# Four more attention units transposed on VectorE and scaled by rows on ScalarE, in a Strassen-type matmul kernel

## The chip, the cores and the metric

The kernel runs on one core of one Trainium2 chip. The metric is the device time of one execution in microseconds (us), as the median of the runs. PE is TensorE, DVE VectorE, ACT ScalarE, POOL GpSimd, SP SyncE, whose queue issues the transfers.

## The reference

The input is attention in blocks of 64 tokens, for 8 batches, 8 heads, 576 tokens and a head of 64, and behind it a two-layer network with a gate:

```
scores = q_c @ k_c.T / 8            # per block of 64 tokens
attn   = softmax(scores)            # rows of 64, minus their maximum
out    = attn @ v_c
x      = out as (4608 tokens, 512)
h      = x @ w_in                   # 512 -> 2048
g      = h * clip(h + 3, 0, 6) / 6
y      = g @ w_out                  # 2048 -> 512
```

All of it is float32. Products are taken in three passes of a split into a high part and a rest (`passes`, lines 376 to 380), so that one tile of 128 x 128 by 512 costs three matmuls.

## The kernel before

The 4608 tokens are nine column blocks of 512 (n = 0 to 8). Attention of one block is two **units**, named by block and half: "30" is block 3, first half. A unit has 16 score matrices of 64 x 64 per pair of lanes, held as 128 lanes x 1024 columns in two PSUM banks.

Blocks 1 and 2, 3 and 4, 5 and 6, 7 and 8 form pairs, and the two matmul layers of a pair (or of the part of it that is not done plainly) use seven products in place of eight, with sums and differences of quarters of the weights and of x (Strassen's method in Winograd's form). Each product of the first layer is called f, of the second s: `f6.0.5` is product 6 of the first layer for the first pair, rows 5. The four sums of quarters of a weight tile are made by `combine` (lines 480 to 482) on DVE: four operations on 256 columns each, the next on the result of the last, for 16 weight tiles (`whole`, `comb`, `top`, `less`, `send`, lines 880 to 884). They are split into a high part and a rest, stored to DRAM and loaded again by later pairs.

The steps of a unit (lines 661 to 694):

- `scores` on PE; a unit's scores follow the product of the unit before it in one piece (`products`).
- `max`: the largest of each row, on DVE.
- Either `less`, `exp`, `sum` (one DVE subtraction, one ACT exponential of 1024 columns, one DVE sum of the rows with a small addition and a reciprocal), or, for the units in `ROWS`, `negate`, `exp0_` to `exp7_`, `invert`: 16 ACT exponentials of 64 columns, each with its own bias and with its sum accumulated.
- `share`: DVE multiplies the 1024 columns with the reciprocals.
- Either `turn` and `turned` (eight transposes of 128 x 128 on PE into PSUM and one ACT copy), or, for the units in `FLIPPED`, `flip`, `save`, `down`, `up`: one DVE transposition in blocks of 32 x 32 from PSUM into SBUF, and five ACT copies of 512 columns that put the blocks in their places (lines 312 to 324). A flipped unit keeps its exponentials in PSUM, in the place of the scores, and its scores are laid out in another order (lines 246 to 252).
- `product` on PE into two banks, then `keep`, an ACT copy of them.

Before the change units 30, 31, 40 and 41 are in `ROWS` and not in `FLIPPED`; unit 21 is in neither.

**The order** is not written by hand: `Schedule.order` (lines 105 to 149) takes all steps with a cost, the steps they depend on and a due time, subtracts from each due time the costs of the steps behind it, and lists them greedily per engine. All engines then issue in this order. The PSUM banks are rings: `h` has two, `o` four. A product of a unit that stands among the f and s products (`PLACES`, line 726) takes both banks of `h`, in a place of the ring that is fixed (unit 30 behind the first group of f products, 31, 40 and 41 behind the first, third and fifth s product). The next product that uses `h` (numbers 6 and 3) waits until these banks are read, that is until the unit's `keep`.

Of the kernel before, what the change touches and what calls it, by code (L numbers as in the profile page):

```python
# [43 lines left out]
LAG = 2  # L44
ROWS = ["30", "31", "40", "41", "60", "61", "80", "81"]
XDVE = ["x0.s0c", "x0.s2", "x0.s2b", "x0.s3", "x0.s3b"]
# [19 lines left out]
LATE = (5, 9)  # L66
FLIPPED = ("50", "51", "60", "61", "70", "71", "80", "81")

# [71 lines left out]
def tile_kernel(ctx: ExitStack, tc: tile.TileContext, qk_in, v_in, weights, out):  # L140
# [84 lines left out]
    class Attention:  # L225
# [67 lines left out]
        def share(self):  # L293
            DVE.tensor_tensor(out=self.flat(self.e), in0=self.flat(self.e), in1=self.wide(self.z), op=ALU.mult)

        def soft(self, step):
            for f in ((self.largest,), (self.lessen, self.exp), (self.total,), (self.share,))[step]:
                f()
# [161 lines left out]
    parked = {}  # L460

    def sum_steps(m, p):
        cols = lambda k: slice(256 * k, 256 * k + 256)
        t = {}

        def q(row, col):
            f, k = quarter(m, row, col)
            return t["a"][:, f, cols(k)]

        def whole():  # L470
            t["a"] = sp.tile([P, 2, 512], F32, name="a")
            for f in range(2):
                if in_dram(m, p):
                    nc.sync.dma_start(out=t["a"][:, f], in_=astore["ab"[m] + str((p + NFP * f) // 2)][:, p % 2])
                else:
                    h, l = [w_of(m, p + NFP * f)[:, k].bitcast(F32) for k in range(2)]
                    DVE.tensor_tensor(out=t["a"][:, f], in0=h, in1=l, op=ALU.add)

        def combine(engine):
            for to, x, y, op in ((q(1, 1), q(1, 0), q(1, 1), ALU.add), (q(1, 0), q(0, 0), q(1, 0), ALU.subtract),  # L480
                                 (q(0, 0), q(1, 1), q(0, 0), ALU.subtract), (q(0, 1), q(0, 1), q(0, 0), ALU.subtract)):
                engine.tensor_tensor(out=to, in0=x, in1=y, op=op)

        def high():
            t["hl"] = parked[m, p] = hp.tile([P, 2, 2, 2, 256], F32R, name="hl")
            t["s"] = t["a"].rearrange("p f (k t) -> p f k t", k=2)
            ACT.copy(out=t["hl"][:, :, :, 0], in_=t["s"])

        def lower(engine):
            engine.tensor_tensor(out=t["hl"][:, :, :, 1], in0=t["s"], in1=t["hl"][:, :, :, 0].bitcast(F32), op=ALU.subtract)  # L490

        def send():
            for i, row, col in ((5, 1, 1), (7, 1, 0), (6, 0, 0), (3, 0, 1)):
                f, k = quarter(m, row, col)
                nc.sync.dma_start(out=kept(m, p, i), in_=t["hl"][:, f, k].rearrange("p l t -> p (l t)").bitcast(F32))

        def send_own():
            for i, row, col in ((1, 0, 0), (2, 0, 1), (4, 1, 1)):
                f, k = quarter(m, row, col)
                to = kept(m, p, i).rearrange("p (l t) -> p l t", l=2)  # L500
                nc.sync.dma_start(out=to, in_=w_of(m, p + NFP * f)[:, :, cols(k)].bitcast(F32))

        return whole, combine, high, lower, send, send_own
# [48 lines left out]
    def x_steps(s):  # L552
        n = NSTD + 2 * s
        b = lambda i, j: xraw[n + j][:, i]
        name = lambda i: f"x{s}.{i}"
        minus = lambda to, x, y, on=DVE: lambda: on.tensor_tensor(out=b(*to), in0=b(*x), in1=b(*y), op=ALU.subtract)
        sub = ("DVE", 1.22)
        ops[s] = {}
        last = name("s0")
        sub_on = lambda k: ("POOL", 2.5) if k in XPOOL else sub  # L560
        steps = [(last, *sub_on("s0"), [], minus((0, 1), (0, 1), (0, 0), POOL if "s0" in XPOOL else DVE), [0, 1])]

# [7 lines left out]
        for i in ORDER_A:  # L570
            reads = {2: [3], 3: [2]}.get(i, [])
            steps.append((name(f"{i}h"), "ACT", 1.05, [last], lambda slot, i=i: high(i, slot), reads))
            steps.append((name(f"{i}l"), "DVE", 1.22, [name(f"{i}h")], lambda i=i: lower(i), []))
            for k, at, to, x, y, reads in (("s1", 5, (0, 1), (1, 1), (0, 1), [2]), ("s2", 6, (0, 0), (0, 1), (0, 0), []),
                                           ("s3", 6, (0, 1), (1, 0), (0, 1), [3])):
                if i == at:
                    steps.append((name(k), *sub_on(k), [name(f"{i}l"), name("1l"), last], minus(to, x, y, POOL if k in XPOOL else DVE), reads))
                    last = name(k)
# [4 lines left out]
    def first_x_steps():  # L583
# [9 lines left out]

        def from_banks(u, i, y):
            def f():
                for (to, part), (less, _) in zip(heads[u].parts(t(i)), heads[u].parts(y())):
                    DVE.tensor_tensor(out=to, in0=part, in1=less, op=ALU.subtract)
            return f
# [12 lines left out]
        of = lambda i: lambda: t(i)  # L611
        work.add("x0.s0", "DVE", 1.22, ["product20", "rest10", "c7", "own6", "own7"], from_banks("20", 5, x(1, 0, 0)), due=due_of["20"])
        work.add("x0.s1", "DVE", 1.38, ["product21", "x0.s0c"], from_banks("21", 6, of(5)), due=due_of["21"])
        for name, i, one, two, kind, after in (("x0.s0c", 5, of(5), x(1, 0, 1), ALU.subtract, ["x0.s0"]),
                                               ("x0.s2", 7, of(6), x(1, 0, 0), ALU.subtract, ["x0.s1", *left(15)]), ("x0.s2b", 7, of(7), x(1, 0, 1), ALU.subtract, ["x0.s2"]),
                                               ("x0.s3", 4, x(1, 1, 0), of(6), ALU.subtract, ["x0.s1", "rest11", *left(15)]), ("x0.s3b", 4, of(4), x(1, 1, 1), ALU.add, ["x0.s3"])):
            on = name not in XDVE
            work.add(name, "POOL" if on else "DVE", 2.7 if on else 1.22, after, op(POOL if on else DVE, i, one, two, kind))
# [14 lines left out]
    def weight_of(p, i):  # L633

        if i in (1, 2, 4):
            return w_of(0, p + NFP * (i == 4))[:, :, 256 * (i != 1):256 * (i != 1) + 256]
        row, col = {5: (1, 1), 7: (1, 0), 6: (0, 0), 3: (0, 1)}[i]
        return parked[0, p][:, row, col]
# [13 lines left out]
    def attention(u, due, scores=(), less=(), keep=(), bank=None):  # L652
# [10 lines left out]
        if u in ROWS:  # L663
            rows = [("negate", "DVE", 0.12, a.negate, ()), *[(f"exp{k}_", "ACT", 0.62, lambda k=k: a.exps(k, e() if k == 0 else None), less if k == 0 and u not in FLIPPED else ()) for k in range(8)],
                    ("invert", "DVE", 0.45, a.invert, ())]
        steps = [("scores", "PE", 1.30, a.scores, ["qk" + u, *scores]), ("max", "DVE", 1.23, a.largest, ()), *rows, ("share", "DVE", 1.22, a.share, ()), *([("flip", "DVE", 1.22, a.flip, less), ("save", "ACT", 0.56, lambda: a.swap(0), ()), ("down", "ACT", 1.0, lambda: a.swap(1), ()), ("up", "ACT", 1.0, lambda: a.swap(2), ())]
                   if u in FLIPPED else [("turn", "PE", 1.07, a.turn, ()), ("turned", "ACT", 1.02, a.turned, ())]), ("product", "PE", 2.26 if after else 1.50, products if after else a.product,
# [196 lines left out]
    for u in [*range(NFP), *range(NFP + NPL, 2 * NFP), *range(NFP, NFP + NPL)]:  # L864
# [5 lines left out]
        work.add(f"whole{u}", *(("SP", 1.57) if in_dram(m, p) else ("DVE", 1.28)), ["room", *work.take("a", 2, f"whole{u}", [f"less{u}s"])], whole)  # L870
        work.add(f"comb{u}", *(("POOL", 4.2, [f"whole{u}"], lambda f=combine: f(POOL)) if u in COMBS else ("DVE", 1.88, [f"whole{u}"], lambda f=combine: f(DVE))))
        work.add(f"top{u}", "ACT", 1.05, [f"comb{u}", *work.take("hl", 2, f"top{u}", [f"send{u}", *last])], high)
        work.add(f"less{u}s", *(("POOL", 2.5, [f"top{u}"], lambda f=lower: f(POOL)) if u in LESS_ON_POOL else ("DVE", 1.22, [f"top{u}"], lambda f=lower: f(DVE))), due=due)
# [34 lines left out]
    def first_product(s):  # L908
# [5 lines left out]
        for p in range(0 if s else NPL, NFP):  # L914
# [5 lines left out]
            for k, i in enumerate(ORDER_A):  # L920
# [48 lines left out]
                elif i in (3, 4):  # L969
# [3 lines left out]
                    if i == 3 and s:  # L973
                        work.add(id_("t1."), "POOL", 1.45, [id_("gate3."), id_("gate2.")], lambda f=gq: POOL.tensor_tensor(  # L974
                            out=f(0, 1), in0=f(0, 1), in1=f(0, 0), op=ALU.subtract))
                        work.add(id_("t2."), "POOL", 1.45, [id_("t1."), id_("gate7.")], lambda f=gq, p=p: POOL.tensor_tensor(  # L976
                            out=t2_of(p), in0=f(1, 1), in1=f(0, 1), op=ALU.subtract))
            place_at(("f", s, p), bank_h)

    def add_units(s):  # L980
# [5 lines left out]
        if s == 0:  # L986
            for p in range(NFP):
# [4 lines left out]
                work.add(f"t2.0.{p}", *(("POOL", 1.45) if TPOOL else ("DVE", 0.69)), [f"t1.0.{p}", f"gate{2 * NFT + NFP + p}" if p < NPL else f"gate7.0.{p}", *free], lambda p=p: (POOL if TPOOL else DVE).tensor_tensor(  # L992
                    out=t2_of(p), in0=gate_of(1, 1, p), in1=gate_of(0, 1, p), op=ALU.subtract))
        made_by = {1: "gate2.", 5: "t1.", 6: "t2.", 2: "gate4.", 3: "gate7."}
        for i in ORDER_B:
            for pp in range(NFP // 2):
# [16 lines left out]
                if i == 5:  # L1013
                    work.add(f"m{s}.7.{pp}", "DVE", 1.22, [f"ul{s}.1.{pp}", *both("t2.", pp)], lambda pp=pp: DVE.tensor_tensor(
                        out=gates_of(0, 0, pp), in0=t2s_of(pp), in1=gates_of(0, 0, pp), op=ALU.subtract))
                elif i == 6:
# [137 lines left out]
```

## Time and profile before

| | |
|---|---|
| runs before | 775.85, 776.64, 776.96 us; median 776.64 |
| profiled execution | 776.96 us, span 775.1 us |
| busy | PE 766.4, DVE 644.4, ACT 432.3, POOL 70.6 us |
| chain that ended last | PE 93%, DVE 3%, DMA 2%, ACT 1% |
| PE transposes (L306) of all units | 80 of 128 x 128 |
| sums of quarters (L482) | 64 on DVE, 27.0 us |

A view by stretches gives, for each stretch of the span, the busy time of each engine. A timeline row gives the start, the duration and the instruction; in brackets stands the idle time of that engine before it and what ended it. PE's matmuls are pipelined, so that the time between two starts, not the duration, is what one costs. On DVE and ACT an instruction may start up to some 0.1 us before the end of the one ahead of it.

### The profile page before, as it was taken

What the parts mean: (1) busy time and instruction counts of PE and PEld (TensorE: products, weight loads), DVE (VectorE), ACT (ScalarE), POOL (GpSimd) and SP (SyncE); (2) the same over time, 40 slices, a digit from 0 to 9 for tenths busy, and PEclk for the clock granted to TensorE, in tenths of its full rate; (3) what the DMA queues carried; (4) which work ended last, traced back from release to release, by engine and by line L of the source; (5) the groups of instructions that cost most, each with busy time, mean ns of one, the idle gap of its engine ahead of it and who ended that gap; (6) DMA issues with size and microseconds to landing.
All of it is one profiled execution on the core that took longest, in us unless ns stands there. A gap on an engine that the chain in (4) does not pass through costs nothing.

```text
span 775.1 us, 14046 instructions
## 1 busy us (share of the span) xinstructions
PE 766.4 (99%) x5538; PEld 628.8 (81%) x5540; DVE 644.4 (83%) x812; ACT 432.3 (56%) x749; POOL 70.6 (9%) x55
## 2 busy tenths in 40 slices
PE   8999999999999999999999999999999999999998
PEld 4788888887888888888888888888888888888887
DVE  6999999999999999967999788678997657679751
ACT  3998843565667654537785535466945333355330
POOL 0000000000000000231300003221200013222000
PEclk9999999999999999999999999999999999999999
DMA  9999999877859997567677785667667666566672
GB/s 369 395 395 342 349 342 319 283 237 232 283 203 334 336 367 266 195 194 255 204 257 248 251 288 191 227 220 261 202 199 232 208 215 198 196 197 204 197 234 92
DMA packets 69426, 198.06 MB, mean 256 GB/s; under 512 B 7024, under 2 KB 19568, under 8 KB 65008
## 3 DMA queue, kind: packets, MB, share of 16 engines
q1 hardware_dynamic: 69216, 197.03, 74.2%
q8 instruction: 44, 0.72, 0.4%
q14 instruction: 22, 0.18, 0.1%
q10 hardware_dynamic: 144, 0.13, 0.1%
HBM read 153.09 MB, written 44.04 MB: 254 GB/s over the span
## 4 chain that ended last, share of the span: by engine, by line
PE 93%; DVE 3%; DMA 2%; ACT 1%; issue 1%; SPq 0%; DVEq 0%; ACTq 0%
PE acc L378 21%; PE acc L379 21%; PE acc L380 21%; PE h L378 8%; PE h L380 8%; PE h L379 8%; PE h L346 2%; PE two L256 1%; PE two L251 1%; PE two L306 1%; DMA b<-hl 1%; DMA out_t<-u 1%; PE h L174 1%; PE two L346 1%; PE h L394 0%
## 5 line engine op out<-in xcount | busy, mean ns | idle before, releaser
L378 PE MATMUL acc<-wa,ws 128*128 128x512 f32 (+1 forms) x536 | 208.8, 390 | 0.1
L380 PE MATMUL acc<-wa,ws 128*128 128x512 f32 (+1 forms) x536 | 207.8, 388 | 0.0
L379 PE MATMUL acc<-wa,ws 128*128 128x512 f32 (+1 forms) x536 | 207.8, 388 | 0.0
L1007 ACT CAST wa<-wb 128x1024 fp32r<-128x1024 f32 x96 | 99.8, 1051 | 74.6 <-PE acc L380 46.1
L1011 DVE TENSOR_TENSOR wa<-wb,wa 128x1024 fp32r<-128x1024 f32 x96 | 120.3, 1271 | 17.7 <-ACT wa L1007 17.5
L378 PEld LDWEIGHTS acc<-wa,ws 128*128 128x128 f32 x536 | 100.7, 188 | 21.7 <-DVE u L900 0.5
L380 PEld LDWEIGHTS acc<-wa,ws 128*128 128x128 f32 x536 | 100.7, 188 | 20.6
L379 PEld LDWEIGHTS acc<-wa,ws 128*128 128x128 f32 x536 | 100.7, 188 | 20.3
L974 POOL TENSOR_TENSOR wb<-wb 128x512 f32<-128x512 f32 x24 | 33.8, 1407 | 628.7 <-DVE wb L788 621.8
L785 ACT ACTIVATE r<-acc,half 128x512 f32<-128x512 f32 x90 | 61.5, 686 | 31.2 <-DVE acc L900 26.8
L785 ACT ACTIVATE r<-h,half 128x512 f32<-128x512 f32 x38 | 26.1, 687 | 91.2 <-DVE h L900 83.9
L788 DVE SCALAR_TENSOR_TENSOR wb<-r,acc 128x512 f32<-128x512 f32 x90 | 61.1, 683 | 6.7 <-ACT r L785 6.2
L379 PE MATMUL h<-wa,ws 128*128 128x512 f32 (+1 forms) x144 | 55.2, 383 | 0.0
L380 PE MATMUL h<-wa,ws 128*128 128x512 f32 (+1 forms) x144 | 55.2, 383 | 0.0
L378 PE MATMUL h<-wa,ws 128*128 128x512 f32 (+1 forms) x144 | 55.2, 383 | 0.0
L900 DVE TENSOR_TENSOR u<-h,p 128x512 f32<-128x512 f32 x32 | 21.9, 686 | 27.7 <-PE h L380 22.7
L900 DVE TENSOR_TENSOR acc<-acc,u 128x512 f32<-128x512 f32 x48 | 33.2, 696 | 6.2 <-PE acc L380 6.2
L976 POOL TENSOR_TENSOR g<-wb,wb 128x512 f32<-128x512 f32 x24 | 36.1, 1504 | 1.9
L788 DVE SCALAR_TENSOR_TENSOR wb<-r,h 128x512 f32<-128x512 f32 x38 | 25.9, 681 | 11.8 <-ACT r L785 11.8
L378 PE MATMUL acc<-wa,wa 128*128 128x512 f32 x88 | 34.9, 397 | 0.2 <-DVE h L900 0.2
L379 PE MATMUL acc<-wa,wa 128*128 128x512 f32 x88 | 34.3, 390 | 0.0
L380 PE MATMUL acc<-wa,wa 128*128 128x512 f32 x88 | 34.3, 390 | 0.0
(211 smaller groups left out, 1420.7 us busy)
## 6 DMA issues: line engine op xcount, KB each, us to landing
ws<-b SPq DMA_DIRECT2D x84, 512.0 KB, 4.7
ws<-a SPq DMA_DIRECT2D x72, 512.0 KB, 4.4
qk<-qk_in SPq DMA_DIRECT2D x17, 1024.0 KB, 7.5
wa<-b SPq DMA_DIRECT2D x28, 512.0 KB, 6.1
a<-wa SPq DMA_DIRECT2D x40, 256.0 KB, 6.2
v<-v_in SPq DMA_DIRECT2D x17, 512.0 KB, 5.3
wa<-w_in_out SPq DMA_DIRECT2D x8, 1024.0 KB, 12.2
wb<-w_in_out SPq DMA_DIRECT2D x8, 1024.0 KB, 9.8
```

The source lines that it names most:

```text
L174: PE.matmul(idle, lhsT=nought.broadcast_to([P, P]), rhs=nought.broadcast_to([P, NT]), start=True, stop=True)
L346: PE.matmul(po[s][o, a, i, :], lhsT=self.v[rows, a, i, o], rhs=self.aT[rows, a, i, o], start=True, stop=True)
L378: PE.matmul(ps, lhsT=a_h, rhs=b_h, start=first, stop=False, skip_group_check=more)
L379: PE.matmul(ps, lhsT=a_h, rhs=b_l, start=False, stop=False, skip_group_check=more)
L380: PE.matmul(ps, lhsT=a_l, rhs=b_h, start=False, stop=last, skip_group_check=more)
L785: ACT.activation(out=t["r"], in_=ps(), func=AF.Relu, bias=half, scale=1.0 / 6.0)
L788: work.add("gate" + name, "DVE", 0.69, ["relu" + name, *more], lambda: DVE.scalar_tensor_tensor(out=out(), in0=t["r"], scalar=1.0, in1=ps( ...
L900: return lambda: DVE.tensor_tensor(out=out(), in0=x(), in1=y(), op=ALU.add)
L974: work.add(id_("t1."), "POOL", 1.45, [id_("gate3."), id_("gate2.")], lambda f=gq: POOL.tensor_tensor(out=f(0, 1), in0=f(0, 1), in1=f(0, 0) ...
L976: work.add(id_("t2."), "POOL", 1.45, [id_("t1."), id_("gate7.")], lambda f=gq, p=p: POOL.tensor_tensor(out=t2_of(p), in0=f(1, 1), in1=f(0, ...
L1007: ACT.copy(out=g_ops[s, i, pp][:, :, 0], in_=src())
L1011: work.add(low, *(("POOL", 2.5) if on else ("DVE", 1.22)), [high], lambda i=i, pp=pp, src=src, on=POOL if on else DVE: on.tensor_tensor(ou ...
```

## The change

Unit 21 joins `ROWS`. Units 30, 31, 40 and 41 join `FLIPPED`. The same four are in a new list `SCALED`: their `share` on DVE is replaced by four steps `scale0_` to `scale3_` on ACT, each of four products of 64 columns with a column of the reciprocals. In `combine` two of the four sums, with other signs, become one operation on 512 columns with one operand repeated; the other two stay at 256 columns, and the three are steps of their own. With the signs, the four sums stand at other quarters (`SUM_AT`), and seven kinds of subtraction or addition elsewhere, on operands of the same shape, change their sign.

```diff
-ROWS = ["30", "31", "40", "41", "60", "61", "80", "81"]
+ROWS = ["21", "30", "31", "40", "41", "60", "61", "80", "81"]
+SCALED = ["30", "31", "40", "41"]
-FLIPPED = ("50", "51", "60", "61", "70", "71", "80", "81")
+FLIPPED = ("30", "31", "40", "41", "50", "51", "60", "61", "70", "71", "80", "81")
...
+        def scale(self, k):
+            for c in range(4 * k, 4 * k + 4):
+                ACT.mul(self.flat(self.e)[:, c], self.flat(self.e)[:, c], self.z[:, c:c + 1])
...
+    SUM_AT = {5: (1, 0), 7: (0, 0), 6: (1, 1), 3: (0, 1)}
...
-        def combine(engine):
-            for to, x, y, op in ((q(1, 1), q(1, 0), q(1, 1), ALU.add), (q(1, 0), q(0, 0), q(1, 0), ALU.subtract),
-                                 (q(0, 0), q(1, 1), q(0, 0), ALU.subtract), (q(0, 1), q(0, 1), q(0, 0), ALU.subtract)):
-                engine.tensor_tensor(out=to, in0=x, in1=y, op=op)
+        def combine(k):
+            if k:
+                to, x = ((1, 1), (0, 0)) if k == 1 else ((0, 1), (1, 1))
+                DVE.tensor_tensor(out=q(*to), in0=q(*to), in1=q(*x), op=ALU.subtract)
+                return
+            four = t["a"].rearrange("p f (k t) -> p (f k) t", k=2)
+            DVE.tensor_tensor(out=four[:, 0:2] if m else four[:, 0:3:2], in0=q(1, 0).unsqueeze(1).broadcast_to([P, 2, 256]), in1=four[:, 0:4:3], op=ALU.subtract)
...
-            for i, row, col in ((5, 1, 1), (7, 1, 0), (6, 0, 0), (3, 0, 1)):
+            for i, (row, col) in SUM_AT.items():
...
-        steps = [..., ("share", "DVE", 1.22, a.share, ()), *([("flip", ...), ("save", ...), ("down", ...), ("up", ...)]
+        steps = [..., *([(f"scale{k}_", "ACT", 0.82, lambda k=k: a.scale(k), ()) for k in range(4)] if u in SCALED else [("share", "DVE", 1.22, a.share, ())]), *([("flip", ...), ...]
...
-        work.add(f"comb{u}", *(... ("DVE", 1.88, [f"whole{u}"], lambda f=combine: f(DVE))))
-        work.add(f"top{u}", "ACT", 1.05, [f"comb{u}", ...], high)
+        work.add(f"comb{u}", "DVE", 0.67, [f"whole{u}"], lambda f=combine: f(0))
+        work.add(f"comb{u}b", "DVE", 0.525, [f"comb{u}"], lambda f=combine: f(1))
+        work.add(f"comb{u}c", "DVE", 0.525, [f"comb{u}b"], lambda f=combine: f(2))
+        work.add(f"top{u}", "ACT", 1.05, [f"comb{u}c", ...], high)
```

## Rows read from the trace of the kernel before

**Rows 1.** The page: busy us of each engine, share, instructions

```profile
PE 766.4 (99%) x5538; PEld 628.8 (81%) x5540; DVE 644.4 (83%) x812; ACT 432.3 (56%) x749; POOL 70.6 (9%) x55
```

**Rows 2.** By stretches: length, busy of PE, PEld, DVE, ACT, POOL, clock, DMA, GB/s

```profile
0.00:30.00 30.00, 25.67 (x400) 16.26 (x403) 20.72 (x24) 17.52 (x22) 0.74 (x7) 1.00 0.95 380
30.00:175.00 145.00, 145.00 (x1126) 119.45 (x1125) 139.69 (x192) 100.22 (x147) 0.00 (x0) 1.00 0.93 328
175.00:180.00 5.00, 4.33 (x30) 2.83 (x32) 4.90 (x10) 2.48 (x3) 0.00 (x0) 1.00 0.61 203
200.00:280.00 80.00, 80.00 (x721) 66.56 (x720) 78.33 (x106) 55.41 (x144) 0.00 (x0) 1.00 0.86 293
```

**Rows 3.** Timeline of PE around the turn of unit 30: start, us, instruction

```profile
174.59 1.03 PE L306 MATMUL two<-ident,e 128*128 128x128 f32 x8
...
175.80 0.50 PE L378 MATMUL acc<-xd,hl 128*128 128x512 f32 x1 [0.18 <-DVE g L900]
```

**Rows 4.** Timeline of PE around the turn of unit 31

```profile
224.37 1.04 PE L306 MATMUL two<-ident,e 128*128 128x128 f32 x8
225.16 0.47 PE L378 MATMUL acc<-wa,wa 128*128 128x512 f32 x1
225.47 0.40 PE L379 MATMUL acc<-wa,wa 128*128 128x512 f32 x1
225.71 0.40 PE L380 MATMUL acc<-wa,wa 128*128 128x512 f32 x1
```

**Rows 5.** Timeline of DVE, unit 21 and one combination of quarters (L482)

```profile
122.91 1.22 DVE L267 TENSOR_TENSOR e<-two,m 128x1024 f32<-128x1024 f32 x1
124.05 1.79 DVE L482 TENSOR_TENSOR a<-a 128x256 f32<-128x256 f32 x4
125.77 1.21 DVE L274 TENSOR_REDUCE z<-e 128x16 f32<-128x1024 f32 x1
127.01 0.18 DVE L275 TENSOR_SCALAR z<-z 128x16 f32<-128x16 f32 x1
...
127.51 1.23 DVE L294 TENSOR_TENSOR e<-e,z 128x1024 f32<-128x1024 f32 x1
```

**Rows 6.** By line: ns min/median/max, first and last start, forms

```profile
L482 DVE TENSOR_TENSOR a<-a x64: 416/425/428, 107.1 to 265.8; 128x256 f32<-128x256 f32 x64
...
L314 DVE STREAM_TRANSPOSE e<-two x8: 1240/1242/1245, 318.4 to 581.4; 128x1024 f32<-128x1024 f32 x8
...
L324 ACT COPY e<-e x16: 615/618/625, 320.3 to 584.6; 32x512 f32<-32x512 f32 x16
```

**Rows 7.** Timeline of ACT, exponentials by rows of unit 30

```profile
154.97 0.31 ACT L286 ACTIVATE e<-two,m 128x64 f32<-128x64 f32 x1
155.16 0.20 ACT L286 ACTIVATION_READ_ACCUMULATOR e<-two,m 128x1 f32 x1
155.26 0.31 ACT L286 ACTIVATE e<-two,m 128x64 f32<-128x64 f32 x1
```

**Rows 8.** Timelines of ACT and PE: keeps of units 30, 31, 41, next h products, unit 40

```profile
180.96 1.07 ACT L359 COPY xa<-h 128x512 f32<-128x512 f32 x2
184.72 0.39 PE L378 MATMUL h<-wa,hl 128*128 128x512 f32 x1
...
230.65 1.07 ACT L359 COPY xa<-h 128x512 f32<-128x512 f32 x2 [1.61 <-PE h L346]
235.70 0.39 PE L378 MATMUL h<-wa,wa 128*128 128x512 f32 x1
...
250.51 1.01 ACT L310 COPY e<-two 128x1024 f32<-128x1024 f32 x1
253.00 1.16 PE L346 MATMUL h<-e,v 64*64 64x64 f32 x64
...
278.21 1.07 ACT L359 COPY xb<-h 128x512 f32<-128x512 f32 x2
285.51 0.39 PE L378 MATMUL h<-wa,wa 128*128 128x512 f32 x1
```

More of the change, by code (lines that the diff above doesn't have):

```diff
@@ L555, in x_steps @@
         name = lambda i: f"x{s}.{i}"
-        minus = lambda to, x, y, on=DVE: lambda: on.tensor_tensor(out=b(*to), in0=b(*x), in1=b(*y), op=ALU.subtract)
+        mix = lambda to, x, y, kind, on=DVE: lambda: on.tensor_tensor(out=b(*to), in0=b(*x), in1=b(*y), op=kind)
         sub = ("DVE", 1.22)
@@ L560, in x_steps @@
         sub_on = lambda k: ("POOL", 2.5) if k in XPOOL else sub
-        steps = [(last, *sub_on("s0"), [], minus((0, 1), (0, 1), (0, 0), POOL if "s0" in XPOOL else DVE), [0, 1])]
+        steps = [(last, *sub_on("s0"), [], mix((0, 1), (0, 1), (0, 0), ALU.subtract, POOL if "s0" in XPOOL else DVE), [0, 1])]
         def high(i, slot):
@@ L573, in x_steps @@
             steps.append((name(f"{i}l"), "DVE", 1.22, [name(f"{i}h")], lambda i=i: lower(i), []))
-            for k, at, to, x, y, reads in (("s1", 5, (0, 1), (1, 1), (0, 1), [2]), ("s2", 6, (0, 0), (0, 1), (0, 0), []),
-                                           ("s3", 6, (0, 1), (1, 0), (0, 1), [3])):
+            for k, at, to, x, y, kind, reads in (("s1", 5, (0, 1), (1, 1), (0, 1), ALU.add, [2]), ("s2", 6, (0, 0), (0, 1), (0, 0), ALU.add, []),
+                                                 ("s3", 6, (0, 1), (1, 0), (0, 1), ALU.subtract, [3])):
                 if i == at:
-                    steps.append((name(k), *sub_on(k), [name(f"{i}l"), name("1l"), last], minus(to, x, y, POOL if k in XPOOL else DVE), reads))
+                    steps.append((name(k), *sub_on(k), [name(f"{i}l"), name("1l"), last], mix(to, x, y, kind, POOL if k in XPOOL else DVE), reads))
                     last = name(k)
@@ L592, in first_x_steps, with from_banks @@
         ops[0] = {}
-        def from_banks(u, i, y):
+        def from_banks(u, i, y, kind):
             def f():
                 for (to, part), (less, _) in zip(heads[u].parts(t(i)), heads[u].parts(y())):
-                    DVE.tensor_tensor(out=to, in0=part, in1=less, op=ALU.subtract)
+                    DVE.tensor_tensor(out=to, in0=part, in1=less, op=kind)
             return f
@@ L611, in first_x_steps @@
         of = lambda i: lambda: t(i)
-        work.add("x0.s0", "DVE", 1.22, ["product20", "rest10", "c7", "own6", "own7"], from_banks("20", 5, x(1, 0, 0)), due=due_of["20"])
-        work.add("x0.s1", "DVE", 1.38, ["product21", "x0.s0c"], from_banks("21", 6, of(5)), due=due_of["21"])
+        work.add("x0.s0", "DVE", 1.22, ["product20", "rest10", "c7", "own6", "own7"], from_banks("20", 5, x(1, 0, 0), ALU.subtract), due=due_of["20"])
+        work.add("x0.s1", "DVE", 1.38, ["product21", "x0.s0c"], from_banks("21", 6, of(5), ALU.add), due=due_of["21"])
         for name, i, one, two, kind, after in (("x0.s0c", 5, of(5), x(1, 0, 1), ALU.subtract, ["x0.s0"]),
-                                               ("x0.s2", 7, of(6), x(1, 0, 0), ALU.subtract, ["x0.s1", *left(15)]), ("x0.s2b", 7, of(7), x(1, 0, 1), ALU.subtract, ["x0.s2"]),
+                                               ("x0.s2", 7, of(6), x(1, 0, 0), ALU.add, ["x0.s1", *left(15)]), ("x0.s2b", 7, of(7), x(1, 0, 1), ALU.add, ["x0.s2"]),
                                                ("x0.s3", 4, x(1, 1, 0), of(6), ALU.subtract, ["x0.s1", "rest11", *left(15)]), ("x0.s3b", 4, of(4), x(1, 1, 1), ALU.add, ["x0.s3"])):
@@ L636, in weight_of @@
             return w_of(0, p + NFP * (i == 4))[:, :, 256 * (i != 1):256 * (i != 1) + 256]
-        row, col = {5: (1, 1), 7: (1, 0), 6: (0, 0), 3: (0, 1)}[i]
+        row, col = SUM_AT[i]
         return parked[0, p][:, row, col]
@@ L665, in attention @@
                     ("invert", "DVE", 0.45, a.invert, ())]
-        steps = [("scores", "PE", 1.30, a.scores, ["qk" + u, *scores]), ("max", "DVE", 1.23, a.largest, ()), *rows, ("share", "DVE", 1.22, a.share, ()), *([("flip", "DVE", 1.22, a.flip, less), ("save", "ACT", 0.56, lambda: a.swap(0), ()), ("down", "ACT", 1.0, lambda: a.swap(1), ()), ("up", "ACT", 1.0, lambda: a.swap(2), ())]
+        steps = [("scores", "PE", 1.30, a.scores, ["qk" + u, *scores]), ("max", "DVE", 1.23, a.largest, ()), *rows, *([(f"scale{k}_", "ACT", 0.82, lambda k=k: a.scale(k), ()) for k in range(4)] if u in SCALED else [("share", "DVE", 1.22, a.share, ())]), *([("flip", "DVE", 1.22, a.flip, less), ("save", "ACT", 0.56, lambda: a.swap(0), ()), ("down", "ACT", 1.0, lambda: a.swap(1), ()), ("up", "ACT", 1.0, lambda: a.swap(2), ())]
                    if u in FLIPPED else [("turn", "PE", 1.07, a.turn, ()), ("turned", "ACT", 1.02, a.turned, ())]), ("product", "PE", 2.26 if after else 1.50, products if after else a.product,
@@ L870, in tile_kernel @@
         work.add(f"whole{u}", *(("SP", 1.57) if in_dram(m, p) else ("DVE", 1.28)), ["room", *work.take("a", 2, f"whole{u}", [f"less{u}s"])], whole)
-        work.add(f"comb{u}", *(("POOL", 4.2, [f"whole{u}"], lambda f=combine: f(POOL)) if u in COMBS else ("DVE", 1.88, [f"whole{u}"], lambda f=combine: f(DVE))))
-        work.add(f"top{u}", "ACT", 1.05, [f"comb{u}", *work.take("hl", 2, f"top{u}", [f"send{u}", *last])], high)
+        work.add(f"comb{u}", "DVE", 0.67, [f"whole{u}"], lambda f=combine: f(0))
+        work.add(f"comb{u}b", "DVE", 0.525, [f"comb{u}"], lambda f=combine: f(1))
+        work.add(f"comb{u}c", "DVE", 0.525, [f"comb{u}b"], lambda f=combine: f(2))
+        work.add(f"top{u}", "ACT", 1.05, [f"comb{u}c", *work.take("hl", 2, f"top{u}", [f"send{u}", *last])], high)
         work.add(f"less{u}s", *(("POOL", 2.5, [f"top{u}"], lambda f=lower: f(POOL)) if u in LESS_ON_POOL else ("DVE", 1.22, [f"top{u}"], lambda f=lower: f(DVE))), due=due)
@@ L976, in first_product @@
                         work.add(id_("t2."), "POOL", 1.45, [id_("t1."), id_("gate7.")], lambda f=gq, p=p: POOL.tensor_tensor(
-                            out=t2_of(p), in0=f(1, 1), in1=f(0, 1), op=ALU.subtract))
+                            out=t2_of(p), in0=f(1, 1), in1=f(0, 1), op=ALU.add))
             place_at(("f", s, p), bank_h)
@@ L992, in add_units @@
                 work.add(f"t2.0.{p}", *(("POOL", 1.45) if TPOOL else ("DVE", 0.69)), [f"t1.0.{p}", f"gate{2 * NFT + NFP + p}" if p < NPL else f"gate7.0.{p}", *free], lambda p=p: (POOL if TPOOL else DVE).tensor_tensor(
-                    out=t2_of(p), in0=gate_of(1, 1, p), in1=gate_of(0, 1, p), op=ALU.subtract))
+                    out=t2_of(p), in0=gate_of(1, 1, p), in1=gate_of(0, 1, p), op=ALU.add))
         made_by = {1: "gate2.", 5: "t1.", 6: "t2.", 2: "gate4.", 3: "gate7."}
@@ L1014, in add_units @@
                     work.add(f"m{s}.7.{pp}", "DVE", 1.22, [f"ul{s}.1.{pp}", *both("t2.", pp)], lambda pp=pp: DVE.tensor_tensor(
-                        out=gates_of(0, 0, pp), in0=t2s_of(pp), in1=gates_of(0, 0, pp), op=ALU.subtract))
+                        out=gates_of(0, 0, pp), in0=t2s_of(pp), in1=gates_of(0, 0, pp), op=ALU.add))
                 elif i == 6:
```

## The prediction

> **What bounds the kernel now.** I read the busy line of the page first, then the stretches, then PE's instructions around its few gaps, then VectorE and ScalarE in the same stretches. TensorE is busy 766.4 of 775.1 us and VectorE 644.4 [rows 1]. The stretches say where the 8.7 idle us are: 4.33 in the first 30 us (before anything here is touched), none from 30 to 175, 0.67 from 175 to 180, none from 200 to 280 [rows 2]; the other 3.7 lie outside these, the tail of the last store among them. The granted clock is 1.00 in each of them, so no term of the sum is one of the clock. From 30 us on the time is thus the sum of what TensorE is given, and another engine counts only where it lets TensorE run dry. VectorE is near that: 78.33 of 80 us between 200 and 280, where ScalarE has 55.41 [rows 2], and the 0.67 us gap is its doing in part: the matmul at 175.80 waits for VectorE's sum of line 900 [rows 3].
>
> **Removed from TensorE.** Units 30, 31, 40 and 41 lose their eight transposes. For unit 31, transposes begin at 224.37 and the next product at 225.16: 0.79 us. The first gap between matmuls after them is 0.31 us (225.16 to 225.47), the next 0.24, so the switch costs another 0.07 to 0.08. A turn is 0.87 us [rows 4]; the units 40 and 41 look alike. Three of them stand in stretches without any gap: 3 x 0.87 = 2.61 us. That of unit 30 at 174.59 lies ahead of a matmul that waits for VectorE until 175.80 anyway [rows 3]: alone its removal gives 0, with VectorE earlier by as much, 0.87. The scores of these units take the other order, same count and size of matmuls; I cost that at nothing. The sign edits turn subtractions into additions of one shape: nothing.
>
> **VectorE.** Per changed unit the share goes (1.23 us, the last row of rows 5) and the flip comes (1.242 [rows 6]): 0 net, four times. Unit 21 goes to exponentials by rows: it loses the subtraction (122.91 to 124.05, 1.14 us) and the sum over columns (125.77 to 127.01, 1.24), keeps the two small operations behind it, and gains one negation of 16 columns, about the 0.2 of 127.01: -2.2 us [rows 5]. A combination is four operations on 256 columns in 1.72 us (124.05 to 125.77 [rows 5]), 0.43 each. Now it is one on 512 and two on 256. No 512-column sum of this shape with a repeated operand is in the trace; the operations on 1024 and on 256 columns bound it. At no gain per column it is 2 x 0.43, and the combination is unchanged; if only columns counted beyond a fixed part, from 0.43 at 256 and 1.14 at 1024 it is 0.43 + 256 x 0.92 ns = 0.67, and the combination is 1.53. I take 0.2 us saved in each of the 16, with 0 and 0.4 (the small ones overlapping other work as independent ones do) as ends: 3.2 us, 0 to 6.4; one operation fewer on the same 1024 columns excludes a loss. They run from 107.1 to 265.8 [rows 6], and by VectorE's timeline nine of the 16 lie ahead of 174 us. So VectorE is 2.2 + 9 x 0.2 = 4.0 us lighter when unit 30 is turned and 5.4 us lighter by 275. TensorE asks for its operands up to 3.5 us earlier there; VectorE gives back more than that. This is why I let the 2.61 us stand in a stretch where VectorE is 98% busy, and why I take unit 30's 0.87 whole and 0.5 of the 0.67 us gap: that sum needs to come only 1.2 us earlier, 175.80 - 174.59.
>
> **ScalarE.** Unit 21: sixteen exponentials at 0.29 us from start to start (154.97 to 155.26 [rows 7]), 4.7 us, in place of one of about 1.1, at a time when ScalarE is at two thirds (100.22 of 145 us [rows 2]). Each of the four units gets sixteen products of 64 columns with a column of factors. The trace has none. From above it is an exponential with its accumulator read, 0.29 us; from below what the exponential holds the engine before that read starts, 0.19 (154.97 to 155.16 [rows 7]). Nothing is accumulated, so I take 0.20, next to the lower end: 3.2 us, 3.0 to 4.7. After the flip come five copies of 512 columns, the longest of 0.618 [rows 6]; with 0.08 of overlap each I take 2.7 us for the five. The copy of the transposes, 1.01 [rows 8], goes. Net +4.9 us a unit, 20 us in all, 15 of them between 200 and 280: 55.4 + 15 = 70 of 80. Busy, not full.
>
> The Trainium skill speaks against both halves. VectorE: DVE Perf Modes, Rules for kernel authors, sends a 128x128 transpose to TensorE, since VectorE's works in 32x32 blocks; ScalarE: Activation LUTs, Rules for kernel authors, sends multiplications to VectorE. In engine time the trace agrees: 0.87 + 1.0 us go and 1.24 + 2.7 come. By them the change would cost time; it would do so here through longer chains, which is the first rival below. But only TensorE's share is on the path. For an activation with one column operand the Trainium skill (ScalarE: Activation LUTs, What ACT_TABLE_LOAD costs) gives 280 ns and 0.833 ns a column, less 93 ns of overlap: an estimate of 0.24 us for 64 columns, 3.8 a unit, by which the chains below would grow by 4.5 and the time would be 774.0.
>
> **What the new chain is up against.** A changed unit's own chain, from maximum to product, grows by 3.2 - 1.2 (scaling) + 1.2 + 2.7 (flip, moves) - 1.0 - 1.0 (transposes, copy) = 3.9 us; with the dear scaling by 5.4. Who waits: the unit's product takes both h banks, and the next product in an h bank stands, with all of TensorE behind it, until the unit is kept. The room has two parts. From the end of the keep to that h product: unit 30, 182.03 to 184.72, 2.7 us; unit 31, 231.72 to 235.70, 4.0; units 40 and 41 together, 279.28 to 285.51, 6.2. And where a product stood ready and waited: unit 40's copy ends at 251.52 and its product starts at 253.00, 1.5 us; unit 30's transposes start at 174.59 and take 1.03, with the copy it is ready at 176.6, with a product of 1.1 at 177.7, but the keep starts at 180.96, 3.2 us; unit 31 by the same steps 227.5 against 230.65, 3.1 [rows 3, 4 and 8]. So the room is 5.9 at unit 30, 7.1 at unit 31, 7.7 for 40 and 41 together, against 3.9, 3.9 and 7.8: enough, by 0.1 at the last. The order is also worked out again with the longer chain subtracted from the due times, which moves a unit's early steps up. I cost the stretch at nothing; the room is its cover.
>
> **The sum.** 776.96 (span 775.1 and 1.9 around it) - 2.61 - 0.87 - 0.5 = 773.0. That execution lies 0.32 above the median of the runs, 776.64; against the median I forecast 772.7. Its own range: with unit 30's turn and the gap both unchanged 774.0, with the whole gap gone 772.5; half a microsecond of new order on either side makes it 772.0 to 774.5.
>
> **Rivals.** With g the growth of a chain, TensorE stands for what g has above 5.9, above 7.1, and 2g above 7.7.
> *Late products (slower).* Place: the first h product behind each unit. A chain of more and shorter steps also queues more: four scaling steps, a flip and three moves for a share, a turn and a copy; where each of the five added hand-overs stands half of a 1.0 us ScalarE operation, g is 3.9 + 2.5 = 6.4, and TensorE stands 0.5 + 5.1 = 5.6 us: 776.6 - 4.0 + 5.6 = 778.2. With the dear scaling too, g = 7.9, it is 2.0 + 0.8 + 8.1 = 10.9 and 783.5. It decides from a growth of 5.8 on, where the whole gain of 4.0 is gone. For it: ScalarE at nearly 90% between 200 and 280. Against: VectorE, where these chains queue most, gets lighter, and the early steps are moved up.
> *Gain eaten (same).* The scaling is dear, g = 5.4 without queueing: 3.1 us at units 40 and 41, 776.6 - 4.0 + 3.1 = 775.7. Or the combinations save nothing, unit 30's turn stays hidden and waits between ScalarE and VectorE cost 1 to 2 us: 776.6 - 2.6 + 1.5 = 775.5. For it: from 200 to 280 VectorE has 1.7 us left [rows 2], so that a wait for a scaled unit is soon passed on.
> *More than forecast.* The new order also closes some of the 4.33 us of the start: 771.5. Little speaks for it, since nothing that is due there changes.
>
> **How the numbers follow.** Forecast 0.62 (772.0 to 774.5); late products 0.10 (777 to 784); gain eaten 0.20 (774.5 to 777); more 0.08 (770.5 to 772). The range that holds 8 in 10 runs from 771.2 to 776.8: it leaves out the slow rival and the ends of the other two. What a measurement can tell from no change is 0.2%, 1.55 us: faster is under 775.1, slower over 778.2. Faster: 0.62 + 0.08 + a quarter of 0.20 = 0.75; slower: most of the slow rival, 0.08; same 0.17.
>
> **What would show it.** Right: no transposes of TensorE after unit 21's; TensorE's busy time down by about 3.5 us and idle after 30 us not above 0.8; VectorE's busy time down by about 5 and ScalarE's up by 20 to 25; the scaling instruction's pitch 0.2 us; the stage that starts at 300 us starting about 4 us earlier and everything behind it shifted whole. Wrong: waits of h products on ScalarE's keep or moves of units 30 to 41, TensorE gaps of a microsecond between 170 and 290, a scaling pitch near 0.3, or a gap at 175 that stays (then unit 30's 0.87 was hidden, as rows 3 allow).

## The result, and the profile after

The changed kernel takes 781.65 us (median of 6 runs, 779.92 to 784.14) against 776.52: a ratio of 1.007, 95% interval 1.0049 to 1.0091. It is slower, by 5 us; 772.7 had been forecast and the range ended at 776.8. The profiled run, the slowest of the six, took 784.14 us with a span of 781.9. Of the runs used below, one of e9 (2884 us) and one of the kernel before (1562 us) took several times as long as the others and are left out.

The busy line and the stretches of the changed kernel, in the columns of [rows 1] and [rows 2]:

```profile
PE 766.5 (98%) x5508; PEld 628.1 (80%) x5508; DVE 638.4 (82%) x795; ACT 464.4 (59%) x860; POOL 70.6 (9%) x55
```

```profile
0.00:30.00 30.00, 25.68 (x404) 16.57 (x405) 21.33 (x25) 18.25 (x22) 0.74 (x7) 1.00 0.94 378
30.00:175.00 145.00, 144.31 (x1119) 118.32 (x1118) 137.36 (x185) 110.54 (x198) 0.00 (x0) 1.00 0.95 336
175.00:180.00 5.00, 4.60 (x34) 3.55 (x38) 5.00 (x9) 2.64 (x5) 0.00 (x0) 1.00 0.23 39
...
200.00:280.00 80.00, 76.55 (x656) 62.81 (x658) 71.52 (x94) 73.18 (x199) 0.00 (x0) 0.98 0.76 259
...
250.00:260.00 10.00, 8.03 (x147) 6.74 (x146) 8.99 (x13) 8.61 (x15) 0.00 (x0) 0.83 0.78 256
...
300.00:310.00 10.00, 7.20 (x29) 5.61 (x28) 7.16 (x9) 3.59 (x5) 0.00 (x0) 0.91 0.67 269
```

TensorE had no gap between 200 and 280; now it is idle 3.45 us there and ScalarE is busy 73.2 us of 80 in place of 55.4. The gaps of TensorE, from its timeline:

```profile
175.40 0.50 PE L383 MATMUL acc<-xd,hl 128*128 128x512 f32 x1 [1.09 <-DVE g L912]
...
252.77 0.33 PE L351 MATMUL h<-e,v 64*64 64x64 f32 x4 [1.70 <-ACT e L329]
253.37 1.66 PE L351 MATMUL h<-e,v 64*64 64x64 f32 x58 [0.27 <-ACT e L329]
...
276.57 0.50 PE L384 MATMUL acc<-wa,wa 128*128 128x512 f32 x1 [0.93 <-DVE wa L1023]
...
308.19 0.68 PE L383 MATMUL acc<-wa,ws 128*128 128x512 f32 x1 [2.80 <-DVE u L912]
```

The account against the kernel before: the turns are gone (48 transposes in place of 80), -3.5 us; idle time between 30 and 770 us is 0.69 + 0.40 + 3.45 + 3.43 = 8.0 in place of 0.8, +7.2; and TensorE's busy time, which should be 766.4 - 3.5 = 762.9, is 766.5, +3.6. The last goes with a lower clock: behind the gap at 252 the granted clock is 0.83 over 10 us, so that part of that stretch ran at 1.2 GHz, and the 58 matmuls at 253.37 take 1.66 us where all 64 of such a product had taken 1.16 [rows 8]; around the gap at 308 it is 0.91 (300 to 310). The sum, 7.3, is what the spans show (6.8) to half a microsecond; the first f product also starts 0.6 earlier. The one run whose mean granted clock was 1.00 took 779.92: without the clock's part the loss is about 3.4 us.

Now to ScalarE, whose timeline shows unit 40's exponentials in place in PSUM, and then its products (L299):

```profile
239.00 0.28 ACT L287 ACTIVATE two<-two,m 128x64 f32<-128x64 f32 x1
239.20 0.20 ACT L287 ACTIVATION_READ_ACCUMULATOR two<-two,m 128x1 f32 x1
239.43 0.29 ACT L287 ACTIVATE two<-two,m 128x64 f32<-128x64 f32 x1
...
242.46 3.82 ACT L299 ACTIVATE two<-two,z 128x64 f32<-128x64 f32 x12
```

From start to start an exponential takes 0.43 to 0.44 us, not the 0.29 of [rows 7], and a product 3.82 / 12 = 0.32, above both ends that had been set (0.19 and 0.29). The chain of a unit has grown by 3.9 + 16 x 0.15 + 16 x 0.12 = 8.2 us.

The order gives these steps 0.62 us for two exponentials and 0.82 for four products (`exp`, `scale`); they take 0.88 and 1.25. What an engine with a fixed order does with that, VectorE's timeline shows at the flips of units 30 and 41:

```profile
170.26 1.25 DVE L319 STREAM_TRANSPOSE e<-two 128x1024 f32<-128x1024 f32 x1 [1.36 <-ACT two L299]
...
274.15 1.25 DVE L319 STREAM_TRANSPOSE e<-two 128x1024 f32<-128x1024 f32 x1 [1.47 <-ACT two L299]
```

VectorE stands 1.36 us before a flip that is not ready, and all that is queued behind it, the sum of line 912 for which TensorE waits at 175.40 among it. At 276.57 TensorE waits for a split of VectorE behind the second of these.

The gap at 308 has another end. VectorE's operation there needs a buffer that a store still reads:

```profile
307.35 0.69 DVE L912 TENSOR_TENSOR u<-acc,u 128x512 f32<-128x512 f32 x1 [2.73 <-DMA out_t<-u]
```

The store was issued behind the loads of unit 50's v and unit 60's q and k, which in the kernel before were issued at 277.80 and 278.70:

```profile
293.80 0.75 SPq L243 DMA_DIRECT2D v<-v_in  x1
294.60 0.55 SPq L238 DMA_DIRECT2D qk<-qk_in  x1
298.91 0.94 SPq L1045 DMA_DIRECT2D out_t<-u  x2
```

The transfers of 285 to 312 us, changed kernel (KB each, median us to landing); in the kernel before the same stores landed in 4.4 us:

```profile
out_t<-u SPq DMA_DIRECT2D x4, 256.0 KB, 7.8
qk<-qk_in SPq DMA_DIRECT2D x1, 1024.0 KB, 11.7
```

### The profile page after: what moved, and what is told of

The parts are those of the page before. It is cut to its first block, busy times and chain, and to the rows that moved or that the text cites. A ratio compares the mean times of both kernels' runs of the same rounds, so it can differ in the third digit from the quotient of the medians.

```text
span 781.9 us, 14072 instructions
## 1 busy us (share of the span) xinstructions
PE 766.5 (98%) x5508; PEld 628.1 (80%) x5508; DVE 638.4 (82%) x795; ACT 464.4 (59%) x860; POOL 70.6 (9%) x55
## 4 chain that ended last, share of the span: by engine, by line
PE 77%; ACT 8%; DVE 7%; DMA 5%; issue 2%; SPq 1%; ACTq 0%; DVEq 0%
PE acc L383 18%; PE acc L384 18%; PE acc L385 18%; PE h L383 6%; PE h L385 6%; PE h L384 6%; ACT two L287 2%; ACT two L299 2%; DMA b<-hl 2%; DMA out_t<-u 2%; ACT wa L1019 2%; DVE wa L1023 1%; PE h L351 1%; PE two L252 1%; PE two L257 1%
## 5 line engine op out<-in xcount | busy, mean ns | idle before, releaser
L287 ACT ACTIVATE two<-two,m 128x64 f32<-128x64 f32 x128 | 36.9, 288 | 7.2 <-PE acc L385 2.8
L384 PE MATMUL acc<-wa,wa 128*128 128x512 f32 x88 | 34.4, 391 | 0.9 <-DVE wa L1023 0.9
L383 PE MATMUL acc<-wa,wa 128*128 128x512 f32 x88 | 34.8, 396 | 0.3 <-ACT wa L1019 0.3
```

Of the source, the lines that this page charges most:

```text
L287: ACT.activation(out=self.flat(self.e)[:, c], in_=self.flat(self.s)[:, c], func=AF.Exp, bias=self.m[:, c:c + 1], scale=SCALE, accum_out=se ...
L383: PE.matmul(ps, lhsT=a_h, rhs=b_h, start=first, stop=False, skip_group_check=more)
L384: PE.matmul(ps, lhsT=a_h, rhs=b_l, start=False, stop=False, skip_group_check=more)
```

## The experiments

Theory A: ScalarE's steps of the four units are longer than the order assumes; the engines stand in their queues for it. Rivals: B, the late loads carry the loss; C, the hand-overs of a longer chain do, whatever ScalarE's work takes; D, the gap at 308 is late work of VectorE and not the transfer; E, the combination or unit 21; F, VectorE is the engine that is short. All of them start from the changed kernel, and each stands against runs of the kernel before on its own chip (776.0 to 776.1). The changed kernel was not timed again there: it counts as 5.1 us slower than the kernel before, and what an edit gives back is the difference of such differences.

**e1_noscale**, the four scaling steps emptied, the order kept:

```diff
         def scale(self, k):
-            for c in range(4 * k, 4 * k + 4):
-                ACT.mul(...)
+            pass
```

> The four units' 16 products by the reciprocals on ScalarE are left out (their output is not scaled), every other instruction keeps its order. Theory A (the chains of units 40 and 41 are too long because 16 exponentials in place in PSUM take 7.0 us and 16 products 5.0): the chains are 5.0 us shorter, TensorE's gaps at 252 and 275 us (2.0 and 1.5) and the lowered clock behind them go, the gap at 305 (2.8) stays, since the loads stand where they stood: 777 us, 775.5 to 778.5. Rival B (the loads of units 50 and 60, late in the queue, carry the loss): nothing much changes, 780 or more. Rival C (hand-overs between the engines, not the size of ScalarE's work): 780 as well, with the gaps at 252 and 275 still over 1 us each.

Measured 777.56 us (773.76 to 779.31, 10 runs), ratio 1.0015 (0.9998 to 1.0031). The gaps at 175, 252 and 275 shrink to 0.3 us or less, one of 1.68 at 303 stays. As A has it, at a loss of 1.5 us in place of 5.1; B and C expected 780. (The edit also takes the wait for the reciprocals out of ScalarE's chain, so that C is tested better by e10.)

**e2_loads**, two loads at the front of SyncE's queue:

```diff
-        load(u, "qk", [scored(prior[u])])
-        load(u, "v", ["product" + prior[u]])
+        load(u, "qk", [scored(prior[u])], first=0 if u == "60" else None)
+        load(u, "v", ["product" + prior[u]], first=0 if u == "50" else None)
```

> Only the loads of unit 50's v and unit 60's q and k go to the front of SyncE's queue (as in the kernel before, right behind unit 41's product). Theory A: only the gap at 305 us goes, with the lowered clock around it: 778 us, 777 to 779.5, gaps at 252 and 275 unchanged. Rival B: the loss of the change goes, 776 or less. Rival D (the gap at 305 is late VectorE work, not the transfer): no change, 781 to 782.

Measured 780.72 us (780.28 to 781.14), ratio 1.0062 (1.0047 to 1.0077). The gap at 308 goes, so D falls, but TensorE now waits 0.98 and 0.59 us for weights (`wa<-b`) at 294 and 297: between 285 and 298 the DMA engines are busy 87% of the time, and 97% in the changed kernel. B falls: the loads as a whole are worth about 0.5 us, which the intervals do not tell from nothing and which is under what A expected.

**e3_sbuf**, exponentials to SBUF and products from there into PSUM, the order kept:

```diff
-                self.e = self.s if self.flipped else ...
+                self.back = f"{self.n}{self.dp}" in SCALED
+                self.e = self.s if self.flipped and not self.back else ...
...
-                ACT.mul(self.flat(self.e)[:, c], self.flat(self.e)[:, c], self.z[:, c:c + 1])
+                ACT.mul(self.flat(self.s)[:, c], self.flat(self.e)[:, c], self.z[:, c:c + 1])
+            if k == 3:
+                self.e = self.s
```

> In units 30, 31, 40 and 41 the exponentials go to SBUF and the products by the reciprocals come back from there into PSUM; the order is the same. Theory A, with the price put down to reading and writing one PSUM tile in a row: exponentials at 0.29 us from start to start as in the kernel before in place of 0.44, products at about 0.2 in place of 0.31, 4 us less a unit; gaps at 252 and 275 mostly gone, that at 305 stays: 777.5 us, 776 to 779. If only the accumulator read behind a PSUM write is dear, exponentials fall to 0.29 and products stay at 0.31: 2.3 us less a unit, 779. Rival C: the pitches fall but the time stays at 780 or more.

Measured 778.51 us (777.39 to 778.97), ratio 1.0031 (1.0018 to 1.0044). This is the expectation's second case. The exponentials are back at 0.29, the products are not shorter (4.17 us for 12):

```profile
166.54 4.17 ACT L300 ACTIVATE two<-e,z 128x64 f32<-128x64 f32 x12
...
239.07 0.38 ACT L288 ACTIVATE e<-two,m 128x64 f32<-128x64 f32 x1
239.27 0.27 ACT L288 ACTIVATION_READ_ACCUMULATOR e<-two,m 128x1 f32 x1
239.36 0.38 ACT L288 ACTIVATE e<-two,m 128x64 f32<-128x64 f32 x1
```

So the exponentials' price is that of writing to PSUM in place of SBUF; whether it needs the source in the same tile was not tried. The products' price does not come from a source in PSUM; a destination in SBUF was not tried for them. VectorE still stands 3.5 us ahead of two flips here, longer than in the changed kernel (2.8).

**e4_costs**, **e15_exp_price** and **e16_scale_price**, the order worked out with the measured prices: both, or one alone:

```diff
-(f"exp{k}_", "ACT", 0.62, ...
+(f"exp{k}_", "ACT", 0.88 if u in FLIPPED else 0.62, ...
-(f"scale{k}_", "ACT", 0.82, ...
+(f"scale{k}_", "ACT", 1.25, ...
```

> The order is worked out again with the measured costs: 0.88 us for two exponentials in PSUM (0.62 was assumed) and 1.25 for four products (0.82). Theory A: the steps in front of the long chains move up, gaps at 252 and 275 fall to half or less: 776.5 us, 773.5 to 779; above the kernel before or not depends on where the loads come to stand. Rival C: as the changed kernel, 780 or more.

> Only the order's price of the exponentials in PSUM is put right (0.88 us for two), that of the products stays at 0.82 for four. Theory A: about half of what both prices give back (5.9 us), since the exponentials are 2.1 us a unit of the 3.8 left out: 778.5 us, 776.5 to 780. If VectorE's stand at the flip behind the products is what counts, little: 780 or more.

> Only the order's price of the products is put right (1.25 us for four), that of the exponentials stays at 0.62 for two. Theory A: 778.5 us, 776.5 to 780. If VectorE's stand at the flip behind the products is what counts, nearly all of it: 777 or less, with no wait of VectorE ahead of a flip.

Both prices: 775.78 us (774.93 to 778.08, 10 runs), ratio 0.9998 (0.9989 to 1.0008): the whole loss goes without one instruction being shorter, though gaps of 0.93 and 0.99 us stay at 252 and 275. The products' price alone: 776.45 (774.77 to 778.38, 10 runs), 1.0003 (0.999 to 1.0016), and VectorE waits ahead of no flip; the exponentials' alone: 779.59 (777.24 to 781.09), 1.0041 (1.0027 to 1.0055), with 2.7 us of such waits. Both give back 5.4 us, the products' 4.7, the exponentials' 1.5, so A's even split was wrong.

That the stand at the flip makes this difference is not shown by the pair. With the exponentials' price alone the 2.7 us are those of units 31 and 41, but TensorE's largest gap, 3.78 us at 178, has no stand at a flip ahead of it: there VectorE waited for the load of a weight tile that it was to combine. An order worked out anew can thus cost some microseconds by where one load and the step that needs it come to stand, and how far that moves the times of the other orders was not measured.

```profile
173.82 0.69 DVE L492 TENSOR_TENSOR a<-a 128x512 f32<-128x512 f32 x1 [1.93 <-DMA a<-wa]
...
178.04 0.50 PE L383 MATMUL acc<-xd,hl 128*128 128x512 f32 x1 [3.78 <-DVE g L912]
```

Over all runs the stand goes with the loss, but its length does not set it. It is 2.6 to 3.5 us in the changed kernel, e2, e3 and the exponentials' price alone, which are 2.4 to 5.1 us slower than the kernel before (e3, with the longest stand, loses least); in the other runs it is 0.3 us or nothing, and they are at most 1.7 us slower. The lines of the flip in the view by source, first with the exponentials' price alone, then with the products':

```profile
its engine sat idle before it (us, times) until:
  ACT two L299: 2.7, 2
```

```profile
L319 DVE STREAM_TRANSPOSE e<-two x12: 1239/1242/1248, 172.7 to 581.7; 128x1024 f32<-128x1024 f32 x12
its engine sat idle before it (us, times) until:
who waited for it (us, times):
  ACT two L329: 6.6, 7
```

**e10_sbuf_costs**, e3's exponentials and right prices (0.62 and 1.30) together:

> All four units; exponentials to SBUF (0.62 for two in the order), products from there into PSUM (1.30 for four). Theory A: 2.3 us less of ScalarE a unit than in the kernel with corrected costs alone, its two gaps of 1 us halve: 774.5 us, 773 to 776. Rival C: as with corrected costs alone, 775.5 to 776.5.

Measured 772.68 us (772.40 to 773.72), ratio 0.9963 (0.9948 to 0.9977). This version beats both kernels. TensorE has 762.0 us of work, 4.4 less than before, and between 200 and 280 no gap, though ScalarE is busy 76 of 80 us:

```profile
PE 762.0 (99%) x5508; PEld 625.4 (81%) x5508; DVE 638.2 (83%) x795; ACT 463.1 (60%) x860; POOL 68.9 (9%) x55
```

```profile
200.00:280.00 80.00, 80.00 (x709) 66.28 (x708) 78.30 (x101) 76.01 (x204) 0.00 (x0) 1.00 0.83 291
```

It keeps every hand-over of the changed kernel: C falls. It has a new order as well as shorter exponentials, and what each gives is not told apart by this run alone; beside both prices alone (775.78) the exponentials, with the order that goes with them, bring about 3 us.

**e12_sbuf_share**, as e10, but VectorE scales (SBUF to PSUM, `SCALED` empty):

```diff
-            DVE.tensor_tensor(out=self.flat(self.e), in0=self.flat(self.e), in1=self.wide(self.z), op=ALU.mult)
+            to = self.s if getattr(self, "back", False) else self.e
+            DVE.tensor_tensor(out=self.flat(to), in0=self.flat(self.e), in1=self.wide(self.z), op=ALU.mult)
+            self.e = to
```

> All four units flipped; exponentials to SBUF, and VectorE in place of ScalarE multiplies by the reciprocals, from SBUF into PSUM (1.22 us a unit). ScalarE gets 5.1 us a unit less, VectorE 1.2 more. Theory A (ScalarE's length decides): gaps go, three turns to four less on TensorE: 773.5 us, 772.5 to 775. Rival F (VectorE is the one that has no room): gaps of TensorE behind VectorE, 776 or more.

Measured 777.61 us (774.57 to 780.91, 10 runs), ratio 1.0021 (1.0002 to 1.0041). F is right here and A is not: ScalarE has 59.55 us of 80, VectorE 78.33, and TensorE waits for it:

```profile
200.00:280.00 80.00, 77.46 (x575) 63.62 (x574) 78.33 (x103) 59.55 (x154) 0.00 (x0) 1.00 0.82 281
```

```profile
278.43 0.50 PE L387 MATMUL acc<-wa,wa 128*128 128x512 f32 x1 [1.83 <-DVE wa L1026]
```

Of these two orders the one with the scaling on ScalarE is 4.9 us faster (772.68 against 777.61).

**e6_noflip**, no new flips, no scaling (`FLIPPED` as before, `SCALED` empty), and **e9_half_costs**, flips and scaling for units 30 and 31 alone, with right prices:

> Units 30, 31, 40 and 41 are turned and scaled as in the kernel before; what is left of the change is unit 21's exponentials by rows, the combination in three operations and the signs. Theory A: no unit's chain is longer than it was where TensorE has no room, no gap over 0.7 us after 30 us, TensorE's work as before: 775.5 us, 774.5 to 776.5. Rival E (the combination in three steps of its own, or unit 21, carries part of the loss): 777.5 or more, with gaps at 175 or 305 as in the changed kernel.

> Only units 30 and 31 are flipped and scaled on ScalarE, 40 and 41 stay as in the kernel before; the order is worked out with the measured costs (0.88 and 1.25). Theory A: two turns less on TensorE (1.74 us) and, since the tight pair is left alone, no gap over 0.7 us: 774.5 us, 773.5 to 775.7. Rival C: hand-overs at 30 and 31 take the gain: 776 or more.

e6: 774.42 us (774.05 to 777.54), ratio 0.9983 (0.9974 to 0.9993); no gap over 0.1 us after 30 us. E falls; the lighter VectorE alone closes the gap at 175, and the whole gains 1.6. e9: 773.46 us (772.46 to 775.65, 7 runs), ratio 0.9971 (0.9958 to 0.9983), with no gap over 0.2 us after 30 us.

**e13_imm**, the products by a constant:

```diff
-                ACT.mul(..., self.z[:, c:c + 1])
+                ACT.mul(..., 0.25)
```

> The changed kernel with its 16 products a unit by a constant in place of the column of reciprocals (their output is scaled by 0.25 and not by the sums). It measures what one product of 64 columns in place in PSUM costs: 0.31 us from start to start if the place sets it, near 0.22 if reading the column of factors does (the Trainium skill, ScalarE: Activation LUTs, What ACT_TABLE_LOAD costs, counts 93 ns for such an operand). At 0.22 a unit's chain is 1.5 us shorter and the time some 779; at 0.31 it is that of the changed kernel, 780 to 784.

One run, 775.75 us. Twelve products take 2.85 to 2.87 us:

```profile
265.32 2.85 ACT L299 ACTIVATE two<-two 128x64 f32<-128x64 f32 x12
```

0.24 us each: 0.08 of the 0.32 is the column of factors. The Trainium skill (ScalarE: Activation LUTs, What ACT_TABLE_LOAD costs) counts 93 ns for it, and the run agrees to about a hundredth of a microsecond. The prediction's estimate from the same section, 0.24 us for a product by a column, is not met: 0.32 was measured, and that decides. The time is 3 us under the expected 779, but lies within the spread of e1, and one run does not settle it. In that run the stand at the flip is 0.3 us and the gap at 252 is gone, though a chain is only 1.3 us shorter.

## Why the prediction was wrong

- *TensorE's work, -3.48 us:* right. 48 transposes are left, and where the clock holds (e10) TensorE has 4.4 us less. The 0.9 beyond the forecast is not the transposes': e6, which keeps all 80, has 1.3 less.
- *VectorE, -5.4 us:* right, -6.0 (644.4 to 638.4). That this closes the gap at 175 is shown by e6; in the changed kernel VectorE's stand at the flip opens it again, 1.09 us.
- *ScalarE, +20 to 25 us:* wrong in size, +32. Two terms of the sum. The products were taken at 0.20 us, next to the lower end; they cost 0.32, over the upper. And the exponentials, which the flip moves into PSUM, were not priced as a change at all: +2.4 us a unit. The trace of before showed that price, since the flipped units of later blocks already had it (0.44 us from start to start): the row was read from a unit that was not flipped.

```profile
349.37 0.29 ACT L286 ACTIVATE two<-two,m 128x64 f32<-128x64 f32 x1 [1.42 <-PE acc L380]
349.58 0.19 ACT L286 ACTIVATION_READ_ACCUMULATOR two<-two,m 128x1 f32 x1
349.81 0.29 ACT L286 ACTIVATE two<-two,m 128x64 f32<-128x64 f32 x1
```

- *The chain, "I cost the stretch at nothing; the room is its cover":* this step failed. The growth was 8.2 us, not 3.9, over the 5.8 that the late-products rival gave as its point, and the order left 3.8 us of it out (2.1 of the exponentials, 1.7 of the products). But nothing stands at that rival's place: no h product waits for a keep. At 252 TensorE stands 1.97 us at unit 40's own product, for ScalarE's last copies (L329). The matmuls behind that product stand with it, so the room up to the next h product was no cover there. At 175 and 276 the loss is made on VectorE: an order worked out with 0.82 for a step of 1.25 puts the flip too early in VectorE's queue, and what is behind it waits, ready or not. That a chain longer than the order assumes makes the loss is shown from both sides: with the products left out and the order kept (e1) 3.7 us come back, with the same instructions and right prices (e4) 5.4. Which share of it goes through VectorE's stand stays open.
- *"The order is also worked out again with the longer chain subtracted":* it was, with too short a chain. With right prices the same step helps: e4 gives back 5.4 us. That e10, with e3's shorter chain besides, measures 772.68 where 772.7 was forecast is in part luck: it is another kernel, the kernel before ran 0.7 us faster on its chip (775.97 against 776.64), and its first f product starts 0.7 us earlier (21.13 against 21.83), which the prediction had only in a rival.
- *Not foreseen:* the order also put two loads behind the weights, and a store behind them held a buffer: 2.8 us at 308, of which moving the loads gives back about 0.5, no more than the noise; and the lower clock behind a gap, 3.6 us in the profiled run. How much of the spread of the changed kernel (779.9 to 784.1) is the clock alone stays open.

## What to carry to other kernels

Where an order is planned ahead, a new kind of step has to be measured before it is planned: a step priced a third too low also costs time on the engine that waits for it, which stands with its whole queue. A price from a trace holds for the place of its operands too, so look for the row with the same source and destination memory, not only the same operation. And where work lands is to be judged by what each engine has left: here the scaling of a unit was dearer on ScalarE (16 x 0.35 = 5.6 us in e10, 1.22 on VectorE in e12), and still was better there, since VectorE had no room.

## What the runs showed of the hardware

- Exponentials of 64 columns with an accumulated sum: 0.29 us from start to start into SBUF, 0.44 in place in PSUM. The difference lies behind the read of the accumulator: from its start to the next exponential 0.10 us ([rows 7]) and 0.23 (239.20 to 239.43).
- Products of 64 columns on ScalarE: 0.24 us by a constant, 0.32 by a column of factors in place in PSUM, 0.35 from SBUF into PSUM (e3).
- Behind gaps of TensorE of 1.70 and 0.27 us at 252 the granted clock was 0.83 over 10 us in the changed kernel; in e2, behind gaps of 1.66 and 0.27 at the same product, it was 1.00.
